# RWKV attention into soft mixture of experts, one core: r, k and v laid out in 256-byte slots, x in a rotating buffer, ku in two buffers, weight loads on another schedule

## Chip, cores, metric

One NeuronCore of a Trainium2 chip. The metric is the device time of one execution in microseconds (us); most executions of a kernel agree within a per cent or two (the kernel before took 167.73 to 170.73 us in its seven runs beside the first experiments). A run is slow when it is over 1.5% above the fastest run of the same kernel; comparisons below use fast runs. A verdict is "unclear" where the interval of the ratio leaves open whether the change is over 2%.

## The reference

Inputs are float32. For each batch b (4), head h (8) and position t (768), with 48 numbers per head:

```python
for t in range(S):
    cur = einsum('bhd,bhe->bhde', u * k[t], v[t])
    y[t] = einsum('bhd,bhde->bhe', r[t], state + cur)
    state = w * state + einsum('bhd,bhe->bhde', k[t], v[t])
x = y.transpose(0, 2, 1, 3).reshape(3072, 384)
logits = x @ phi                      # 8 experts x 4 slots = 32 columns
d = softmax over tokens; slot_input = d.T @ x
slot_out[e] = relu(slot_input[e] @ w1[e]) @ w2[e]      # 384 -> 1024 -> 384
out = softmax over slots(logits) @ slot_out
```

r, k and v are 4.7 MB each; w1 and w2 together 25 MB.

## The kernel before

Tokens go through in 24 chunks of 128 (six per batch). The program text orders each engine's work; step i does the attention of chunk i and prepares chunk i+2. The parts that matter:

```python
ld = ctx.enter_context(tc.tile_pool(name="ld", bufs=2))       # two batches in flight
def load_batch(b):
    tiles = [ld.tile([P, H, nC, D], f32, name=name, tag=name) for name, _ in srcs]
    if b > 0:                                                  # one transfer each for r, k, v
        nc.sync.dma_start(out=t[:].rearrange("p h c d -> p (h c) d"),
                          in_=src[b].rearrange("h (c p) d -> p (h c) d", p=C))
        return
    for c in range(nC): ...                                    # batch 0: one per chunk

def mults(i):
    b, c = divmod(i, nC)
    if c == 1 and 1 <= b < B - 1: load_batch(b + 1)
    nc.gpsimd.tensor_mul(rr[:, :, 0:D], r_b[:, :, c, :], W_neg[:])
    nc.gpsimd.tensor_mul(kk[:, :, 0:D], k_b[:, :, c, :], W_k3)
    ku = wk3.tile([P, H, D], f32, name="ku")                   # three buffers
    nc.gpsimd.tensor_mul(ku[:], k_b[:, :, c, :], u3)
    nc.scalar.copy(v_bf[:], v_b[:, :, c, :])                   # the cast of v

for i in range(nN + 3):
    att_a(i); mults(i + 2); trans(i + 1); att_b(i); r_copy(i + 1)   # guards cut
    xt(i - 1); disp(i - 2); att_c(i); diag(i + 1); lg(i - 1)
    ...
    for n, at in enumerate(W_AT):                              # weights, on GpSimd's queue
        if at == i: load_w(W_ORDER[n])
```

`diag` has VectorE multiply ku by r and sum it, which frees that ku buffer. `r_copy` is the last reader of a batch's r. After the steps come the experts (PE and VectorE) and the output.

The softmax here doesn't subtract the row's maximum and nothing guards it: scores larger than these inputs give would overflow.

## Time and profile before

| stage | from, us | to, us | what sets its end |
|---|---|---|---|
| batch 0, start | 0 | 24.4 | last v of batch 0 lands |
| until V1 | 24.4 | 46.8 | v of batch 1 lands |
| until V2 | 46.8 | 74.1 | v of batch 2 lands |
| until V3 | 74.1 | 106.1 | v of batch 3 lands |
| last steps | 106.1 | 135.8 | VectorE, 3.5 us per step |
| experts | 135.8 | 151.6 | PE, and the last weights |
| output | 151.6 | 168.9 | output transfers |

Measured time: 168.49 us, median of 2 runs. How to read the profile: a line of the stretch view has the stretch, its length, the busy time and instruction count of PE, its weight loads, VectorE (DVE), ScalarE (ACT) and GpSimd (POOL), then the granted PE clock, the busy share of the 16 transfer engines (over 1 where records overlap) and the GB/s written. A line of the wait view has who waited, for whom, us in total, times, and the longest. Lines of the chain are start, duration, what. SPq is SyncE issuing transfers.

### The profile page before, as it was taken

To read this page: it belongs to the slowest core of one execution; us is meant where nothing else is said; L and a number is where in the kernel's file an instruction comes from. 1 tells how busy PE (TensorE), PEld (TensorE's weight loads), DVE (VectorE), ACT (ScalarE), POOL (GpSimd) and SP (SyncE) were. 2 spreads that over 40 slices of the span, in tenths; PEclk is the share of its full clock that TensorE was granted. 3 is DMA by queue.
4 is the path that set the end of the run, shared out by engine and by line. 5 is a ranking of instruction groups with operands and counts; after the bars stand their busy time and mean duration, and the time that the engine had idled before them with its cause. 6 is when DMAs were issued, how large, how long until landed. Compare 5 with 4: busy or idle time off the path is not lost.

```text
span 168.9 us, 3607 instructions
## 1 busy us (share of the span) xinstructions
PE 86.8 (51%) x1433; PEld 65.6 (39%) x1433; DVE 93.7 (55%) x198; ACT 77.9 (46%) x163; POOL 84.2 (50%) x97
## 2 busy tenths in 40 slices
PE   0004898700037787507887810377776576844410
PEld 0003576500036665406765600265554476831000
DVE  2006889900047899607989910379999242215550
ACT  0294659200076888047777400769875400004550
POOL 2009999408912699964469794158993000000000
PEclk9999999975555799975569995589999655555555
DMA  3999999999999799999979999969999999905995
GB/s 73 200 194 193 175 207 181 197 202 222 166 165 201 157 186 196 234 206 206 215 149 189 218 216 202 200 83 140 180 146 160 204 210 204 198 15 209 353 356 201
DMA packets 48592, 32.13 MB, mean 190 GB/s; under 512 B 20160, under 2 KB 45504, under 8 KB 48576
## 3 DMA queue, kind: packets, MB, share of 16 engines
q1 hardware_dynamic: 35952, 18.88, 55.1%
q0 software_dynamic: 11520, 12.58, 46.2%
q10 hardware_dynamic: 1104, 0.44, 1.4%
q8 instruction: 11, 0.18, 0.5%
q14 instruction: 5, 0.04, 0.1%
HBM read 39.77 MB, written 4.72 MB: 263 GB/s over the span
## 4 chain that ended last, share of the span: by engine, by line
DMA 40%; SPq 24%; DVE 11%; PE 11%; ACT 5%; issue 5%; ACTq 0%; DVEq 0%
DMA v_b<-in_v_dram 32%; SPq L61 15%; SPq L66 9%; DMA out_dram<-o_s 5%; PE so_p L349 3%; PE h_p L337 3%; DMA r_b<-in_r_dram 3%; DVE at_s L210 3%; ACT t_s L196 2%; DVE o_s L381 2%; DVE sd_p L183 2%; DVE ku L179 2%; DVE dv L185 2%; ACT xt_s L257 1%; ACT r_p L173 1%
## 5 line engine op out<-in xcount | busy, mean ns | idle before, releaser
L163 POOL TENSOR_TENSOR kk<-k_b,w_rep 128x384 bf16<-128x384 f32 x24 | 24.0, 1000 | 19.2 <-PE sd_p L232 11.8
L179 DVE TENSOR_TENSOR ku<-ku,r_p 128x384 f32<-128x384 f32 x24 | 13.2, 549 | 35.4 <-ACT r_p L173 34.5
L196 ACT COPY t_s<-t_p 128x1024 bf16<-128x1024 bf16 x24 | 24.3, 1012 | 17.0 <-PE t_p L193 17.0
L210 DVE TENSOR_TENSOR at_s<-at_p,mask_ut 128x512 bf16<-128x512 f32 x48 | 30.7, 682 | 0.0
L165 POOL TENSOR_TENSOR ku<-k_b,u_rep 128x384 f32<-128x384 f32 x24 | 24.0, 1000 | 12.5 <-DVE sd_p L183 12.5
L162 POOL TENSOR_TENSOR rr<-r_b,W_neg 128x384 bf16<-128x384 f32 x24 | 24.1, 1003 | 11.6 <-ACT W_neg L100 10.5
L167 ACT CAST v_bf<-v_b 128x384 bf16<-128x384 f32 x24 | 12.1, 506 | 34.3 <-DMA v_b<-in_v_dram 34.2
L264 PE MATMUL xl_p<-phi_s,xt_s 128*128 128x32 bf16 x72 | 6.0, 186 | 39.2 <-ACT xt_s L257 39.1
L264 PEld LDWEIGHTS <-xt_s 128*128 128x128 bf16 x72 | 3.5, 101 | 41.7 <-ACT xt_s L257 41.7
L193 PE MATMUL t_p<-ident,rr 128*128 128x128 bf16 x96 | 11.6, 257 | 13.3 <-POOL rr L162 13.3
L383 ACT ACTIVATE o_s<-o_p,rsum_r 128x384 f32<-128x384 f32 x12 | 6.8, 581 | 23.5 <-PE o_p L377 17.7
L183 DVE TENSOR_REDUCE sd_p<-ku 128x8 f32<-128x384 f32 x24 | 13.5, 561 | 0.8
L185 DVE TENSOR_TENSOR dv<-v_bf,sd_p 128x384 bf16<-128x384 bf16 x24 | 13.3, 553 | 0.8
L257 ACT COPY xt_s<-xl_p 128x384 bf16<-128x384 bf16 x24 | 11.5, 481 | 4.0 <-PE xl_p L255 3.9
L193 PEld LDWEIGHTS <-rr 128*128 128x128 bf16 x96 | 6.6, 111 | 16.5 <-POOL rr L162 13.3
L244 PE MATMUL y_p<-v_bf,at_s 128*128 128x48 bf16 x192 | 12.2, 194 | 1.7 <-DVE at_s L210 1.5
L219 PE MATMUL y_p<-dv,ident 128*128 128x384 bf16 x24 | 9.7, 406 | 6.3 <-DVE dv L185 6.2
L206 PE MATMUL at_p<-t_s 64*128 64x128 bf16 x192 | 11.4, 251 | 1.2 <-ACT t_s L196 1.1
L236 DVE TENSOR_TENSOR st<-sd_p,wm 128x384 bf16<-128x384 f32 x20 | 11.0, 551 | 1.6 <-PE sd_p L232 1.5
L193 PE MATMUL t_p<-ident,kk 128*128 128x128 bf16 x96 | 11.7, 258 | 0.4 <-POOL kk L163 0.4
L246 ACT CAST x_sb<-y_p 128x384 bf16<-128x384 f32 x24 | 11.7, 486 | 0.3 <-PE y_p L244 0.3
L173 ACT COPY r_p<-r_b 128x384 f32<-128x384 f32 x24 | 11.7, 489 | 0.0
(63 smaller groups left out, 170.4 us busy)
## 6 DMA issues: line engine op xcount, KB each, us to landing
w_all<-in_moe_w_dram POOLq DMA_DIRECT2D x16, 768.0 KB, 11.2
out_dram<-o_s SPq DMA_DIRECT2D x12, 384.0 KB, 2.5
r_b<-in_r_dram SPq DMA_DIRECT2D x6, 192.0 KB, 4.9
k_b<-in_k_dram SPq DMA_DIRECT2D x6, 192.0 KB, 4.6
v_b<-in_v_dram SPq DMA_DIRECT2D x6, 192.0 KB, 4.6
w_rep<-in_w_dram ACTq DMA_DIRECT2D x1, 192.0 KB, 4.0
u_rep<-in_u_dram ACTq DMA_DIRECT2D x1, 192.0 KB, 5.7
phi_f<-in_moe_phi_dram ACTq DMA_DIRECT2D x1, 48.0 KB, 5.5
```

Source lines behind the costliest of these rows:

```text
L61: nc.sync.dma_start(out=t[:].rearrange("p h c d -> p (h c) d"), in_=src[b].rearrange("h (c p) d -> p (h c) d", p=C))
L66: nc.sync.dma_start(out=t[:, :, c, :], in_=src[b, :, c * C:(c + 1) * C, :].rearrange("h p d -> p h d"))
L162: nc.gpsimd.tensor_mul(rr[:, :, 0:D], r_b[:, :, c, :], W_neg[:])
L163: nc.gpsimd.tensor_mul(kk[:, :, 0:D], k_b[:, :, c, :], W_k3)
L165: nc.gpsimd.tensor_mul(ku[:], k_b[:, :, c, :], u3)
L173: nc.scalar.copy(r_p[:], loads[b][0][:, :, c, :])
L179: nc.vector.tensor_mul(s["ku"][:], s["ku"][:], s["r_p"][:])
L183: nc.vector.tensor_reduce(d, s["ku"][:], axis=mybir.AxisListType.X, op=ALU.add)
L185: nc.vector.tensor_mul(dv[:], s["v"][:], d[:, :, None].to_broadcast([P, H, D]))
L193: nc.tensor.transpose(t_p[:, a, q, :], s[nm][:, 2 * q:2 * q + 2, :].rearrange("p h d -> p (h d)"), ident[:])
L196: nc.scalar.copy(t_s[:], t_p[:])
L210: nc.vector.tensor_mul(at_s[:, a, :, :], at_p[a][:], mask_ut[:, None, :].to_broadcast([P, nP, P]))
```

## The change

The apparent intent: a row of 48 floats is 192 B; put each in a slot of 256 B of SBUF, the on-chip memory, so that it does not lie across a 256 B boundary. The larger load tiles need room, which comes from x (four chunks in place of 24) and from one ku buffer. The weight loads move to one per step from step 9 on.

```diff
-        tiles = [ld.tile([P, H, nC, D], f32, name=name, tag=name) for name, _ in srcs]
+        tiles = [ld.tile([P, H, nC, 64], f32, name=name, tag=name) for name, _ in srcs]
-                nc.sync.dma_start(out=t[:].rearrange("p h c d -> p (h c) d"),
+                nc.sync.dma_start(out=t[:].rearrange("p h c d -> p (h c) d")[:, :, 0:D],
-            ku = wk3.tile([P, H, D], f32, name="ku")
+            ku = wk.tile([P, H, D], f32, name="ku")          # wk has two buffers
-            nc.scalar.copy(x_sb[:, i, :], y_p[:])
+            x_t = wk4.tile([P, Dm], bf, name="x_t")          # wk4 has four
+            x_of[i] = x_t
+            nc.scalar.copy(x_t[:], y_p[:])
-        W_AT = [3, 5, 8, 10, 11, 14, 16, 17, 18, 19, 20, 21, 22, 23, 24, 24]
+        W_AT = [4, 7, 9, 10, 11, 12, 13, 14, 15, 16, 17, 18, 19, 20, 21, 22]
+    late.close()        # the load tiles' pool ends ahead of the experts
```

(Every read of r, k, v takes `0:D` of the slot; readers of `x_sb` take `x_of[i]`.)

More of the change, by code (lines that the diff above doesn't have):

```diff
@@ L50 @@
     cst = ctx.enter_context(tc.tile_pool(name="cst", bufs=1))
-    ld = ctx.enter_context(tc.tile_pool(name="ld", bufs=2))
+    late = ExitStack()
+    ld = late.enter_context(tc.tile_pool(name="ld", bufs=2))
     loads = {}
@@ L65, in load_batch @@
             for t, (_, src) in zip(tiles, srcs):
-                nc.sync.dma_start(out=t[:, :, c, :],
+                nc.sync.dma_start(out=t[:, :, c, 0:D],
                                   in_=src[b, :, c * C:(c + 1) * C, :].rearrange("h p d -> p h d"))
@@ L125 @@
     st_t = [cst.tile([P, nP, D2], bf, name=f"st{i}") for i in range(2)]
-    x_sb = cst.tile([P, nN, Dm], bf, name="x_sb")
     w1_all = cst.tile([P, E, nM, F], bf, name="w1_all")
@@ L148 @@
          tc.tile_pool(name="wk3", bufs=3) as wk3, \
+         tc.tile_pool(name="wk4", bufs=4) as wk4, \
          tc.tile_pool(name="ps", bufs=1, space=bass.MemoryType.PSUM) as ps, \
@@ L161, in mults @@
             rr, kk = rr_t[i % NB], kk_t[i % NB]
-            nc.gpsimd.tensor_mul(rr[:, :, 0:D], r_b[:, :, c, :], W_neg[:])
-            nc.gpsimd.tensor_mul(kk[:, :, 0:D], k_b[:, :, c, :], W_k3)
-            ku = wk3.tile([P, H, D], f32, name="ku")
-            nc.gpsimd.tensor_mul(ku[:], k_b[:, :, c, :], u3)
+            nc.gpsimd.tensor_mul(rr[:, :, 0:D], r_b[:, :, c, 0:D], W_neg[:])
+            nc.gpsimd.tensor_mul(kk[:, :, 0:D], k_b[:, :, c, 0:D], W_k3)
+            ku = wk.tile([P, H, D], f32, name="ku")
+            nc.gpsimd.tensor_mul(ku[:], k_b[:, :, c, 0:D], u3)
             v_bf = wk3.tile([P, H, D], bf, name="v_bf")
-            nc.scalar.copy(v_bf[:], v_b[:, :, c, :])
+            nc.scalar.copy(v_bf[:], v_b[:, :, c, 0:D])
             st8[i] = dict(rr=rr, kk=kk, ku=ku, v=v_bf)
@@ L172, in r_copy @@
             r_p = ps.tile([P, H, D], f32, name="r_p")
-            nc.scalar.copy(r_p[:], loads[b][0][:, :, c, :])
+            nc.scalar.copy(r_p[:], loads[b][0][:, :, c, 0:D])
             st8[i]["r_p"] = r_p
@@ L236, in att_b @@
                 nc.vector.tensor_mul(st_t[(i + 1) % 2][:], s_p, wm[:])
+        x_of = {}
         def att_c(i):
@@ L254, in xt @@
             for mi in range(nM):
-                nc.tensor.transpose(xl_p[:, mi * P:(mi + 1) * P], x_sb[:, i, mi * P:(mi + 1) * P], ident[:])
+                nc.tensor.transpose(xl_p[:, mi * P:(mi + 1) * P], x_of[i][:, mi * P:(mi + 1) * P], ident[:])
             xt_s = wk.tile([P, nM, P], bf, name="xt_s")
@@ L269, in disp @@
             for mi in range(nM):
-                nc.tensor.matmul(un_p[:, mi, :], x_sb[:, i, mi * P:(mi + 1) * P], Lexp[:, i, :],
+                nc.tensor.matmul(un_p[:, mi, :], x_of[i][:, mi * P:(mi + 1) * P], Lexp[:, i, :],
                                  start=(i == 0 and mi == 0), stop=False, skip_group_check=True)
```

## The prediction

A window is 256 B of SBUF starting at a multiple of 256 B; how many a row touches is counted from the addresses in the built program. That each window costs the same is the estimate from the first batch: 18.5 ns for rows with 2 windows and 13.9 for rows with 1.5 on average, 9.3 ns per window in both. The sum came to 190 us; of the 6 taken off to reach 184, 3 are for the mixed stretches and the rest for doubt. That reads may be a bound of their own is supposition, put at the 13.9 ns of the odd chunks.

> **What bounds the kernel now.** I read the page first (chain, queues), then the waits, the chain in order of time, the stretches by stage, and last the issue times of the first batch.
>
> The page says that the path runs through transfers, not through an engine: no engine is busy over 55% of the span, and the chain that ended last is DMA and its queue for 64%.
>
> ```profile
> DMA packets 48592, 32.13 MB, mean 190 GB/s; under 512 B 20160, under 2 KB 45504, under 8 KB 48576
> q1 hardware_dynamic: 35952, 18.88, 55.1%
> q0 software_dynamic: 11520, 12.58, 46.2%
> DMA 40%; SPq 24%; DVE 11%; PE 11%; ACT 5%; issue 5%; ACTq 0%; DVEq 0%
> ```
>
> q1 carries r, k, v and the output, q0 the expert weights; together they fill the 16 engines. The packet counts tell the sizes. A head's row is 192 B. Batch 0 has 3x8x768 = 18432 rows and they are nearly all of the 20160 packets under 512 B. Batches 1 to 3 have 55296 rows, yet only 25344 packets lie between 512 B and 2 KB, which is 55296/4 = 13824, plus 8192 of the second weights, 3072 output and 256 broadcast packets, exactly. So the later batches write four neighbouring rows as one 768 B packet.
>
> The wait view and the chain name the three stalls: ScalarE's cast of v for the first chunk of each batch.
>
> ```profile
> ACT v_bf L167 <- DMA v_b<-in_v_dram: 34.2, 3, 16.1
> ```
> ```profile
> 29.11 17.63 DMA v_b<-in_v_dram
> ...
> 56.97 17.08 DMA v_b<-in_v_dram
> ...
> 86.72 19.34 DMA v_b<-in_v_dram
> ...
> 142.24 1.61 issue
> ...
> 147.42 1.80 issue
> ```
>
> v lands at V1 = 46.75, V2 = 74.05, V3 = 106.06. That cast stands ahead of the copy of r of an older chunk (r_copy), which frees the buffer for the next batch; so the next r load is issued 2 us after v lands (48.76, 76.07), and batches come strictly one after the other. The two "issue" pieces are PE in the expert stage, waiting for the last weights.
>
> ```profile
> 0.00:24.40 24.40, 8.72 (x88) 6.01 (x89) 10.82 (x29) 12.28 (x22) 13.30 (x22) 1.00 1.11 172
> 24.40:46.80 22.40, 7.56 (x121) 5.83 (x119) 8.67 (x16) 5.07 (x11) 14.51 (x16) 0.76 1.09 195
> 46.80:74.10 27.30, 17.17 (x256) 13.08 (x256) 20.00 (x39) 16.60 (x36) 19.41 (x21) 0.81 1.04 191
> 74.10:106.10 32.00, 17.88 (x255) 14.18 (x255) 19.70 (x37) 16.55 (x36) 20.47 (x22) 0.71 1.11 200
> 106.10:135.80 29.70, 19.25 (x305) 14.51 (x305) 23.32 (x48) 20.67 (x46) 16.53 (x18) 0.84 1.03 159
> 135.80:151.60 15.80, 11.33 (x387) 10.89 (x388) 3.97 (x19) 0.00 (x0) 0.00 (x0) 0.50 0.96 158
> ```
>
> The reader is to see the last two columns: DMA share about 1 or above (records overlap) and about 190 GB/s in every stage up to V3. So V3 is the sum of what the engines have moved by then; after it come 29.7 us of attention bound by VectorE (a step each 3.5 us), 15.8 of experts, 17.3 of output.
>
> The first batch, one 1024-row transfer per issue of SyncE, shows what a row costs:
>
> ```profile
> 9.88 0.79 SPq L66 DMA_DIRECT2D k_b<-in_k_dram  x1
> 10.71 0.72 SPq L66 DMA_DIRECT2D v_b<-in_v_dram  x1
> 11.48 1.19 SPq L66 DMA_DIRECT2D r_b<-in_r_dram  x1
> 12.71 1.13 SPq L66 DMA_DIRECT2D k_b<-in_k_dram  x1
> 13.89 1.14 SPq L66 DMA_DIRECT2D v_b<-in_v_dram  x1
> 15.07 0.94 SPq L66 DMA_DIRECT2D r_b<-in_r_dram  x1
> 16.05 0.84 SPq L66 DMA_DIRECT2D k_b<-in_k_dram  x1
> 16.94 0.85 SPq L66 DMA_DIRECT2D v_b<-in_v_dram  x1
> ```
>
> Three fast, three slow, three fast: it goes by chunk. The landings agree: even chunks 1.18 us per transfer, odd ones 0.89, that is 18.5 and 13.9 ns per row and engine (64 rows per engine).
>
> [...] The built program puts r, k and v at addresses that leave 96 on division by 256. Even chunks then write rows at offsets 96 and 224 (both straddle: 2 windows), odd ones at 32 and 160 (1 and 2: 1.5 on average). 18.5/2 = 9.3 and 13.9/1.5 = 9.3 ns: the trace agrees with one cost per window. The later batches run at 242 packets of 768 B per us when alone, 66 ns each on 16 engines or 16.5 per row. If each row of a packet is written for itself, offsets 96, 32, 224, 160 make 7 windows, 9.4 ns each: agrees again. [...] At 66 to 68 us the trace has 151 load and 150 weight packets per us[...]; but while a first weight (2048 B packets) runs, at 36 to 39, the loads all but stop, 3 to 24 packets per us. [...] Batch 0 with 192 B packets moves 15.7 ns per row, no worse than the later batches' 16.5, so this trace shows no loss by packet size itself.
>
> **The change part by part.**
>
> 1. Slots. The intent is a row that never straddles. But 256 B slots help only if the tile starts well, and the changed program's r, k and v start at 135520, 160096, 184672 and so on: all leave 96 again. Every row then covers 96 to 288, two windows. By 9.3 ns per window, a row costs 18.6 ns everywhere. Later batches: 384 rows per engine and transfer x 18.6 = 7.14 us against 384 x 16.5 = 6.34, +0.8 x 9 transfers = +7.2 us. Batch 0: nine odd transfers x (1.18 - 0.89) = +2.6. Together +9.8 us, all in front of V3.
>
> 2. Rows per packet fall from 4 to 1 in batches 1 to 3. [...] The sum of work stays[...].
>
> 3. Weight loads by step, from 3, 5, 8, 10, 11, 14, 16, 17, 18 ... to 4, 7, 9, 10, 11, 12, ... 22. They stand in GpSimd's order behind the products of chunk step+2. Before, weights 0 to 5 and nearly all of 6 were done by V3. After, weights 4 to 8 belong to chunks 13 to 17, all of which are prepared before V3, and weight 9 follows chunk 18, whose k lands one transfer (6 to 7 us) before V3; its issue comes about 2 us after k (as at 94.58 to 96.63), so it also cuts in. A weight takes 3.7 to 3.9 us (384 packets at 103 per us, 1024 at 265). From 6.8 to 10 weights: 3.2 x 3.8 = +12 us before V3. Given back: the expert stage no longer waits, -(1.6 + 1.8) = -3.4.
>
> 4. Gap after V2. Before, weights filled the 3.7 us between v landing and first bytes of the next r. Now weight 3 goes before V2 and weight 4 is issued some 4 us after it: up to +3.5 us. Weight 0 does fill the gap after V1.
>
> 5. ku with two buffers: chunk i+2's product waits for VectorE's sum of chunk i, a step of 3.5 us before it is needed; nothing on the path. x in four buffers: overwritten by chunk i+4, last read at step i+2; no wait. Engine instructions keep shape and count (GpSimd 1.00 us, casts 0.5), as the instruction order confirms. GpSimd with a weight at each step has 3 x 0.96 + 0.95 = 3.8 us per step against 3.5 of VectorE; over the last 6 steps that is about 2 us, mostly inside its lead.
>
> Sum: 168.5 + 9.8 + 12 + 3.5 - 3.4 = 190. The mixed stretches are cheaper than added up (151/242 + 150/265 = 1.19 us of lone work per us); replayed on the kernel before, plain adding overshoots V3 by about 3 us. And weight 9 may come too late (-4)[...]. I take 184.
>
> **The rivals.**
>
> A. Rows are aligned in effect, or a slot costs one window: the write side gives 9.3 ns and the read side, at the 13.9 of the odd chunks, becomes the bound. Then 9 x 1.0 + 9 x 0.29 = -11.6 us in loads, against +12 + 3.5 - 3.4 of weights: about 169, a draw; if reads allowed 9.3 ns too, 3456 x 4.6 ns = 16 us less, about 153. For it: the intent, and a weight schedule that suits fast loads. Against it: the addresses, and the slow even chunks.
>
> B. The even-odd rhythm comes from the source address (24 KB steps per chunk). Then loads stay as they are and only the weights' order counts: 168.5 + 12 + 3.5 - 3.4 = 180.6, less the 3 for mixing, 177.
>
> C. Weights arrive early and the loads are no longer last: V3 unchanged, -3.4: 165. Against it: loads stop while weights run.
>
> **Range and chances.** Main theory 60% (176 to 194), B 20% (172 to 183), A and C 20% (153 to 172). Predicted 184 us, range 170 to 195; faster by over 2% 0.10, within 2% 0.08, slower by over 2% 0.82.
>
> **What would show it.** No 768 B load packets are left: some 41000 packets more. Load rate alone in batches 1 to 3 near 165 GB/s for step 1 (B: 186; A: over 210). The first batch loses its rhythm: all issues 1.2 us. ScalarE's wait for v grows from 34 to over 45 us, V3 goes to about 125. Ten weights land before V3 and the "issue" gaps of the expert stage are gone. I am wrong if the rows run at 14 ns or less, or if V3 stays near 106.

## The result

186.84 us (186.43 and 187.26) against 168.49: ratio 1.109, interval 1.091 to 1.127, slower. Ratios here and below are the mean time of one kernel's fast runs over that of the other's of the same rounds, so not quite the ratio of the medians quoted. The profiled run spans 184.7 us.

The page of the changed kernel: the packet counts, the queue of r, k, v and the output, and GB/s in 40 slices of 4.6 us.

```profile
GB/s 95 187 167 159 166 170 162 142 163 163 191 147 156 174 187 209 206 214 55 181 185 230 231 228 226 235 223 43 111 210 181 193 167 166 9 7 124 359 351 190
DMA packets 48593, 32.13 MB, mean 174 GB/s; under 512 B 20160, under 2 KB 45504, under 8 KB 48576
q1 hardware_dynamic: 35952, 18.88, 54.0%
```

The counts below 2 KB are those of before to the unit, and so is the queue's: loads of batches 1 to 3 still go in 768 B packets. The 55 and the 43 in the GB/s line are gaps after V2 and after V3.

The chain of the changed kernel, its three long transfers of v:

```profile
33.63 15.79 DMA v_b<-in_v_dram
...
59.23 24.36 DMA v_b<-in_v_dram
...
94.05 30.62 DMA v_b<-in_v_dram
```

Start plus duration gives V1 = 49.4, V2 = 83.6, V3 = 124.7, against 46.75, 74.05 and 106.06 (the prediction shows these lines of the kernel before). Of the 15.8 us between the two spans, 18.6 have accrued by V3, 0.6 more come in the last steps, the experts give back 3.9, and the output takes 0.5 more. The stretches, cut at those points:

```profile
0.00:27.40 27.40, 10.95 (x121) 7.89 (x121) 13.47 (x33) 14.56 (x26) 16.22 (x25) 1.00 1.12 157
27.40:49.40 22.00, 5.07 (x88) 3.77 (x86) 6.09 (x12) 3.09 (x8) 8.07 (x9) 0.69 1.04 161
49.40:83.60 34.20, 17.17 (x256) 13.08 (x256) 19.98 (x39) 16.61 (x36) 19.95 (x21) 0.75 1.08 186
83.60:124.70 41.10, 17.94 (x255) 14.21 (x255) 19.69 (x37) 16.55 (x36) 22.50 (x24) 0.67 1.08 199
124.70:155.00 30.30, 20.18 (x305) 15.33 (x305) 23.53 (x48) 20.64 (x46) 17.73 (x19) 0.78 0.99 155
155.00:166.90 11.90, 10.96 (x387) 10.73 (x388) 3.86 (x19) 0.00 (x0) 0.00 (x0) 0.50 0.16 26
```

The first two stretches are mostly loads: 157 and 161 GB/s where before had 172 and 195 (the latter with more of a weight in it), at about the same full share of the engines (1.12 and 1.04, before 1.11 and 1.09). The experts take 11.9 us at a transfer share of 0.16: the last weight lands at 158.3, and they no longer wait for one.

Loads alone, with no weight on the engines, in batch 1: first the kernel before, then the changed one.

```profile
32.00:35.00 3.00, 1.41 (x25) 1.06 (x25) 1.54 (x3) 0.00 (x0) 0.27 (x1) 1.00 1.12 187
```
```profile
37.00:43.00 6.00, 0.00 (x0) 0.00 (x0) 0.00 (x0) 0.00 (x0) 0.27 (x1) 0.50 1.11 163
```

A row's time on one engine is 192 B x 16 / rate: 16.4 ns at 187 GB/s, 18.8 at 163. The issue times of SyncE in the first batch of the changed kernel:

```profile
16.19 1.14 SPq L67 DMA_DIRECT2D r_b<-in_r_dram  x1
17.38 1.14 SPq L67 DMA_DIRECT2D k_b<-in_k_dram  x1
18.57 1.14 SPq L67 DMA_DIRECT2D v_b<-in_v_dram  x1
19.75 1.14 SPq L67 DMA_DIRECT2D r_b<-in_r_dram  x1
```

The rhythm of three fast, three slow is gone; every chunk goes at the slow pace. These are ScalarE's wait for v, summed over six waits (34.2 us before), and GpSimd's wait ahead of ku, in the changed kernel and then (ku alone) in the one before:

```profile
ACT v_bf L168 <- DMA v_b<-in_v_dram: 54.3, 6, 20.2
...
POOL ku L166 <- DVE sd_p L184: 30.6, 5, 12.0
```
```profile
POOL ku L165 <- DVE sd_p L183: 12.5, 3, 6.1
```

The second was not predicted. Its longest piece, in the order of GpSimd's work, holds back a weight (L142 issues it), which goes out only after V2:

```profile
73.79 1.00 POOL L164 TENSOR_TENSOR kk<-k_b,w_rep 128x384 bf16<-128x384 f32 x1
86.81 1.00 POOL L166 TENSOR_TENSOR ku<-k_b,u_rep 128x384 f32<-128x384 f32 x1 [12.02 <-DVE sd_p L184]
87.75 0.94 POOL L142 DMA_DIRECT2D w_all<-in_moe_w_dram  x1
```

### The profile page after: what moved, and what is told of

Its sections match the earlier page's. It is cut to its first block, busy times and chain, and to the rows that moved or that the text cites. A ratio compares the mean times of both kernels' runs of the same rounds, so it can differ in the third digit from the quotient of the medians.

```text
span 184.7 us, 3621 instructions
## 1 busy us (share of the span) xinstructions
PE 87.1 (47%) x1433; PEld 66.3 (36%) x1433; DVE 93.9 (51%) x198; ACT 78.2 (42%) x163; POOL 84.5 (46%) x97
## 2 busy tenths in 40 slices
DMA packets 48593, 32.13 MB, mean 174 GB/s; under 512 B 20160, under 2 KB 45504, under 8 KB 48576
## 4 chain that ended last, share of the span: by engine, by line
DMA 46%; SPq 23%; PE 11%; DVE 8%; ACT 6%; issue 3%; ACTq 0%; DVEq 0%
DMA v_b<-in_v_dram 38%; SPq L62 14%; SPq L67 9%; DMA out_dram<-o_s 5%; PE h_p L343 3%; PE so_p L355 3%; ACT t_s L197 3%; DMA r_b<-in_r_dram 3%; DVE at_s L211 2%; DVE o_s L387 2%; PE t_p L194 1%; DVE sd_p L184 1%; ACT xt_s L262 1%; DVE dv L186 1%; DVE ku L180 1%
## 5 line engine op out<-in xcount | busy, mean ns | idle before, releaser
L389 ACT ACTIVATE o_s<-o_p,rsum_r 128x384 f32<-128x384 f32 x12 | 6.8, 580 | 19.8 <-PE o_p L383 14.5
L194 PE MATMUL t_p<-ident,kk 128*128 128x128 bf16 x96 | 11.9, 261 | 0.4 <-POOL kk L164 0.4
L251 ACT CAST x_t<-y_p 128x384 bf16<-128x384 f32 x24 | 11.7, 486 | 0.3 <-PE y_p L247 0.3
L174 ACT COPY r_p<-r_b 128x384 f32<-128x384 f32 x24 | 11.7, 488 | 0.0
```

The lines of the kernel that those rows point to most:

```text
L194: nc.tensor.transpose(t_p[:, a, q, :], s[nm][:, 2 * q:2 * q + 2, :].rearrange("p h d -> p (h d)"), ident[:])
```

## The experiments

Theory, an estimate from the first batch of the kernel before: a row costs 9.3 ns per 256 B window it touches in SBUF, and the slots, which start at offset 96, touch two each; weights served ahead of V3 add to that. Rivals: the stride or the packets of the slots cost, not the offset; the source address makes the even-odd rhythm; the weights did it all. The first four ran on one chip, beside the kernel before (168.81 us there).

**Slots alone (a1_slots_only).** The changed kernel with the old schedule; ku still has two buffers.

```diff
-        W_AT = [4, 7, 9, 10, 11, 12, 13, 14, 15, 16, 17, 18, 19, 20, 21, 22]
+        W_AT = [3, 5, 8, 10, 11, 14, 16, 17, 18, 19, 20, 21, 22, 23, 24, 24]
```

> The slots with the old weight schedule. Window theory (each 256 B window a row touches costs 9.3 ns; all rows straddle): load packets 75 ns instead of 66, batch 0 at 1.19 us per transfer in every chunk, no rhythm; 9 x 0.85 + 9 x 0.29 = about +10 us, so 177 to 180 us. Rival (the weights did it all): 168 to 170 us, load packets at 242 per us.

Measured: 185.25 us, ratio 1.0925 (1.083 to 1.102). Loads at 213 packets per us and 1.2 us per transfer in batch 0, as expected, but some 6 us slower than expected. In the trace the transfer engines stood nearly still from 50.9 to 55.0 (share 0.02, 6 GB/s), around V1 (51.6), and the second weight was issued at 55.72 in place of 43.33. That points to ku, and led to two of the next experiments.

**Weights alone (a2_weights_only).** The kernel before with the new `W_AT`.

> The kernel before with only the new weight schedule. If the weights carry their share: V3 (landing of v of batch 3) later by two to three weights, the gaps in the expert stage gone, 174 to 178 us, loads still at 242 packets per us. If slots alone did it: 167 to 169 us.

Measured: 173.81 us, ratio 1.024 (1.016 to 1.033; slower, though unclear whether by 2%), just below the expected range; loads still at 242 packets per us. V3 is at 112.0, 6 us later; nine weights had landed by then instead of six (by bytes moved, 9.4 instead of 6.9); the experts took 10.4 us from their first to their last matmul instead of 14.2. So the schedule costs, but a third of what the prediction gave it (12 + 3.5 - 3.4). And no gap follows V2, at 73.8: with three ku buffers the weight that the changed kernel holds back is issued ahead of it, and the engines stay full from 73.8 to 78.

```profile
69.13 0.99 POOL L165 TENSOR_TENSOR ku<-k_b,u_rep 128x384 f32<-128x384 f32 x1
70.06 0.94 POOL L142 DMA_DIRECT2D w_all<-in_moe_w_dram  x1
```
```profile
73.80:78.00 4.20, 1.84 (x20) 1.49 (x21) 2.14 (x4) 3.17 (x7) 0.98 (x2) 0.50 1.17 208
```

**The changed kernel with aligned slots (a3_slots_at_0).** 160 B of padding ahead of the load tiles moves them from offset 96 to 0.

```diff
         so_r = cst.tile([P, Dm], bf, name="so_r")
+        cst.tile([P, 40], f32, name="pad")
```

> The changed kernel with 160 B of padding ahead of the load tiles, so that every slot starts at a multiple of 256 B. Window theory: one window per row to write, then reads bound at 14 ns or less per row: packets 56 ns or less (at least 285 per us), batch 0 at 0.9 us or less in every chunk; 9 x 1.8 + 18 x 0.3 = -21 us against the changed kernel, 160 to 168 us. Rival (the stride of the slots itself, or the source address, costs): no change, 185 to 188 us.

Measured: 165.34 us, ratio to before 0.968 (0.957 to 0.979); two of the four runs, the profiled one among them, slow. One unused tile takes over 20 us off the changed kernel: the straddle is the main cause, and neither the stride nor the source address.

**The kernel before with aligned rows (a4_rows_at_0).** The same padding line in the kernel before: dense rows, now at 0, 192, 128, 64.

> The kernel before with the same padding, so its dense rows lie at offsets 0, 192, 128, 64. Window theory: 1, 2, 2, 1 windows, 1.5 on average and the same in even and odd chunks: the rhythm of batch 0 goes, all at about 0.89 us, later packets 56 ns (285 per us); 9 x 0.9 + 9 x 0.29 = -10 us, 157 to 161 us. Rival (rhythm from the source address): rhythm and 168.5 us stay.

Measured: 159.53 us, ratio 0.942 (0.934 to 0.950). The rhythm of batch 0 is gone and loads run at 285 packets per us. The gain that aligned slots bring (9.1% in b2 below) is thus more than half to be had without slots. This refutes the source address, which did not move.

The next four ran together (before: 170.31 us).

**Two ku buffers alone (b1_ku2_only).** The kernel before with one line of the change.

```diff
-            ku = wk3.tile([P, H, D], f32, name="ku")
+            ku = wk.tile([P, H, D], f32, name="ku")
```

> The kernel before with ku in two buffers instead of three, nothing else. Theory 2 (two buffers of ku hold GpSimd back at each batch border, and with it the weight loads that stand behind it, so the engines' gap after V1 is no longer filled): the second weight issues after V1 instead of at 43, a gap of 3 to 4 us after V1, 171 to 175 us. Theory 1 (as in the prediction, ku is off the path): 168 to 169.5 us.

Measured: 173.26 us, ratio 1.018 (1.009 to 1.026; slower, though unclear whether by 2%). The order of GpSimd's work shows how; first this kernel, then the one before:

```profile
41.02 0.99 POOL L163 TENSOR_TENSOR kk<-k_b,w_rep 128x384 bf16<-128x384 f32 x1
49.82 1.00 POOL L165 TENSOR_TENSOR ku<-k_b,u_rep 128x384 f32<-128x384 f32 x1 [7.81 <-DVE sd_p L183]
50.76 0.80 POOL L140 DMA_DIRECT2D w_all<-in_moe_w_dram  x1
```
```profile
41.44 0.99 POOL L163 TENSOR_TENSOR kk<-k_b,w_rep 128x384 bf16<-128x384 f32 x1
42.39 0.99 POOL L165 TENSOR_TENSOR ku<-k_b,u_rep 128x384 f32<-128x384 f32 x1
43.33 0.80 POOL L140 DMA_DIRECT2D w_all<-in_moe_w_dram  x1
```

With two buffers, ku of chunk 7 waits for VectorE's sum of chunk 5, which waits for v of batch 1. The weight load behind it in program order waits as well, and the engines stand nearly still for 3.9 us around V1 (46.6):

```profile
46.10:50.00 3.90, 1.05 (x15) 0.82 (x16) 1.34 (x3) 3.17 (x7) 0.18 (x1) 0.50 0.02 6
```

V3 comes 1.2 us later than before, and the last weight, for which the experts wait, lands at 151.4 instead of 149.5.

**Slots that straddle, ku with three buffers, old schedule (b3_slots_ku3_oldw).** Room comes from one buffer less each of x and of its transpose.

```diff
-            ku = wk.tile([P, H, D], f32, name="ku")
+            ku = wk3.tile([P, H, D], f32, name="ku")
-         tc.tile_pool(name="wk4", bufs=4) as wk4, \
+         tc.tile_pool(name="wk4", bufs=3) as wk4, \
-            xt_s = wk.tile([P, nM, P], bf, name="xt_s")
+            xt_s = wk.tile([P, nM, P], bf, name="xt_s", bufs=1)
         ... and W_AT as in the kernel before
```

> Slots that straddle, old weight schedule, ku back in three buffers (room from one buffer less each of x and of its transpose, both not waited for). Theory 2: the surplus of the slots-only run goes, about +10 to +12 us of loads remain, 178 to 181 us, gap after V1 filled. Theory 1 with a larger price of the slots: stays at 184 to 186 us.

Measured: 180.91 us, ratio 1.065 (1.056 to 1.075): the slots alone, about +11 us. The gap after V1 has shrunk to 0.5 us.

**Slots at offset 64 (a5_slots_at_64).** The changed kernel with the old schedule and 224 B of padding: a row covers 64 to 256.

> Changed kernel, old weight schedule, slots at offset 64: a row ends exactly at 256. Window theory: one window, 39 ns per packet of four rows (410 per us), as at offset 0; time 150 to 160 us. Rival (it needs alignment to 256 or 128 B, or the address alone): 66 to 75 ns per packet, 175 to 185 us.

Measured: 159.01 us, ratio 0.936 (0.929 to 0.942), loads at 400 to 415 packets per us. Here a row needed no aligned start: ending at the boundary, it loads at 315 GB/s, where slots at 0 have 319 and slots at 96 have 163 (table below).

**Aligned slots, three ku buffers, old schedule (b2_slots_at_0_ku3_oldw).** The edit of b3 and the 160 B pad together.

> Slots at offset 0, old weight schedule, three buffers of ku: one window per row, and only about 7 weights before V3. V3 near 84, then 59 to 63 us: 143 to 150 us, the fastest so far. If loads were still last in every batch in spite of 39 ns per packet, 153 to 158 us.

Measured: 154.59 us, ratio 0.909 (0.901 to 0.916), correct: faster than both kernels. It misses the expected 143 to 150: V3 came at 88.7, not 84, and the experts, as before, waited for weights (1.7 and 2.4 us in the chain), whose last landed at 133.3. ScalarE's wait for v shrank from 34.2 to 18.4 us:

```profile
ACT v_bf L168 <- DMA v_b<-in_v_dram: 18.4, 2, 10.3
```

This reads as if the sum of loads and weights through to the last weight were now the bound, and not the loads up to V3; c3 and d2 below test it.

Loads alone in four kernels, one line each: dense rows at 0, slots at 64, slots at 0 with three ku buffers, and the next experiment.

```profile
25.00:26.00 1.00, 0.80 (x19) 0.59 (x16) 0.93 (x2) 1.00 (x3) 1.00 (x2) 1.00 1.10 220
```
```profile
36.50:38.00 1.50, 0.00 (x0) 0.00 (x0) 0.00 (x0) 0.00 (x0) 0.00 (x0) 0.50 1.08 315
```
```profile
37.00:39.00 2.00, 0.00 (x0) 0.00 (x0) 0.00 (x0) 0.00 (x0) 1.98 (x3) 0.50 1.10 319
```
```profile
37.00:40.00 3.00, 0.00 (x0) 0.00 (x0) 0.00 (x0) 0.00 (x0) 2.74 (x4) 0.50 1.28 262
```

| rows in SBUF | windows per row | GB/s | ns per row and engine | ns per window |
|---|---|---|---|---|
| slots at 96 (changed) | 2 | 163 | 18.8 | 9.4 |
| dense at 96 (before) | 1.75 | 187 | 16.4 | 9.4 |
| dense at 0 | 1.5 | 220 | 14.0 | 9.3 |
| slots at 64 | 1 | 315 | 9.8 | 9.8 |
| slots at 0 | 1 | 319 | 9.6 | 9.6 |

One cost per window, 9.3 to 9.8 ns, fits all five. Windows of 128 B do not fit: dense rows at 0 would then cost the same as slots at 0 (two windows for every row in both), and they took 14.0 ns against 9.6.

Batch 0 is not in the table, and does not follow it. From v of one chunk to v three chunks on, nine transfers, SyncE took 0.89 us per transfer with slots at 0 (issues at 10.17 and 18.16) and 0.92 with dense rows at 0 (9.94 and 18.19): about 14 ns per row with 1 window and with 1.5. Something other than the windows sets this pace; what, no run shows.

**Source rows 256 B apart (c1_source_256).** b2 with a wrong result: the source address steps 64 floats per partition, so that source rows don't straddle either.

```diff
-                                  in_=src[b].rearrange("h (c p) d -> p (h c) d", p=C))
+                                  in_=bass.AP(tensor=src.tensor, offset=src.offset + b * H * S * D,
+                                              ap=[[64, P], [5696, nC * H], [1, D]]))
         ... and batch 0 likewise
```

> Slots at offset 0, three ku buffers, old weights, and a wrong result on purpose: rows are read from source addresses 256 B apart instead of 192 B, so each source row lies in one window too. If only the window on the write side counts: still about 400 to 415 packets per us, 39 ns, and about 154 us. If the straddling source rows (1.5 windows on average) held part of the 39 ns: over 430 packets per us.

Measured: 157.45 us (ratio 0.935, 0.927 to 0.942, beside another set of runs of the kernel before), loads at 262 GB/s where b2 has 319: slower than b2, not equal and not faster. The packets changed, which neither expectation had:

```profile
DMA packets 90064, 32.13 MB, mean 209 GB/s; under 512 B 75456, under 2 KB 86976, under 8 KB 90048
```

75456 - 20160 = 55296: each row of batches 1 to 3 now is a packet of 192 B. So the 768 B packets of the other kernels go by the source, where rows of neighbouring tokens lie side by side, and neighbouring tokens go to neighbouring partitions; the layout in SBUF did not change the count (20160 packets under 512 B with dense rows, with slots at 96 and with slots at 0). A single-row packet costs 11.7 ns where a row of a joint packet costs 9.6. Whether a straddling source row costs anything stays open, because the edit changed both. Why batch 0 goes in 192 B packets, although its source rows lie side by side too, is open as well.

**One weight earlier (c3_one_weight_earlier, d1_slots_at_0_again, d2_one_earlier_again).** c3 is b2 with `W_AT = [3, 5, 6, 8, 10, 11, 14, 16, 17, 18, 19, 20, 21, 22, 23, 23]`; then b2 (d1) and c3 (d2) again side by side.

> Slots at offset 0, three ku buffers, old weight schedule with one weight more issued at step 6, where the engines have some 4 us of idle time between 42 and 57 us, and the two last ones at step 23. If the end is set by the sum of the engines' work: last weight lands 2 to 4 us earlier, 151 to 153 us. If the earlier weight only delays v of batch 2: 154 to 158 us.

Measured: 151.04, 151.29, 154.07 and 162.77 us, the latter two slow; ratio of the fast ones to before 0.895, unclear.

> The same kernel as the aligned one with three ku buffers and the old schedule, again, beside the next on the same chip: 153 to 156 us.

Measured: 155.65 us, ratio 0.920 (0.915 to 0.925).

> The same kernel with one weight at step 6, whose profile fell in the slow state the first time. If the idle time of the engines was worth a weight: 1.5 to 3 us faster than its neighbour, last weight landing 2 to 4 us earlier. If the first difference was chance: within 1 us.

Measured: 154.86 us median; the six runs are 150.43 and five from 153.36 to 155.17, which count as slow because of the one at 150.43. The earlier weight is not shown to help. The profiles do show the last weight landing at 132.4 us instead of 136.2, as expected; the times point the same way, but fast against fast rests on one run.

## Why the prediction was right

Time (184 against 186.84) and direction held, and so did the main mechanism, slots that straddle. Of the other four steps two were wrong, one was over-priced, and one came true for another reason. By its steps:

1. **Slots.** Held. Predicted +9.8 us from 18.6 ns per row; measured 18.8 ns and, alone, +11.0 (6.5% of 170). The load rate it named, near 165 GB/s, is 163; V3, named at about 125, is 124.7. Rival A needed aligned addresses; given those by padding, the rows of batches 1 to 3 took 9.6 ns, the lower of its two cases, and not the 13.9 of the other. Rival B fell with the padded kernel before.
2. **Rows per packet fall from 4 to 1.** Wrong. The counts stayed, and some 41000 further packets never came. That four rows go in one packet follows the source (c1); what a packet costs follows the offsets of its rows in SBUF, 163 to 319 GB/s with the same packets. The 7 windows for four rows fit the table, at 9.4 ns each. The trace of the kernel before has 151 load and 150 weight packets per us with 768 B weight packets, 3 to 24 load packets with 2048 B ones, and no run shows why.
3. **Weights.** Right in kind, too large in size: +12 and -3.4, so +8.6, against +4.1 measured alone (2.4% of 169). The count was nearly right: by bytes, 9.8 weights had moved by V3 in the changed kernel and 9.4 in the weights-only run, against 6.9. The price was not: there, 2.5 weights of 3.8 us moved V3 by 6.0 us. Stretches in which loads and weights run together, allowed 3 us in the sum, may be the rest; it was not taken apart. The return in the experts, -3.4 predicted, is -3.9 in the stretches.
4. **Gap after V2.** It came, 2.4 us without a packet (84.6 to 87.0), but not from the schedule. The weight that could have filled it stood behind a ku that waited 12.0 us for one of its two buffers. From the kk before it, an estimate without that wait is issue at about 75.7, 8 us ahead of V2; in the weights-only run, same schedule with three buffers, it went ahead of V2 and there was no gap. So this gap belongs to step 5, and that 3.5 us was near is luck. No run has the whole change with three ku buffers; this is read from the two traces.
5. **ku off the path.** Wrong. The step looked at who needs ku, and not at what stands behind it in GpSimd's order: a weight load. Alone it costs +3.0 us (1.8% of 170), with its gap at V1; in the changed kernel another weight is under way there, and the gap lies after V2. C, that weights come early and loads are not last, is refuted by the weights-only run.

Two of its readings of batch 0 were also less than they seemed. The odd chunks' 13.9 ns, divided by 1.5 windows, gave the same 9.3 ns as the even ones; but rows of one window were no faster there (see below the table), so that agreement proves little. And its own 18.5 and 13.9 ns average to 16.2 per row, not 15.7; that packet size costs nothing is not borne out by 11.7 against 9.6 ns in c1.

The sum came out near in part by luck: weights 4.5 us too high, slots 1 too low, a gap of 3.5 put down to the schedule where ku alone costs 3.0, and 6 taken off for mixing and doubt. Measured parts multiply to 1.065 x 1.018 x 1.024 = 1.110, against 1.109 for the whole change; since the gap of ku lies elsewhere in the whole, the match is closer than the parts warrant.

## What to carry to other kernels

Here padding an inner dimension to 256 B helped only where the tile's base lay well (9.6 and 9.8 ns per row at offsets 0 and 64, 18.8 at 96): read the base address out of the built program, and check whether rows cross a multiple of 256. One unused 160 B tile was worth 5.8% in the kernel before, and with slots and three ku buffers 14.5% (180.91 to 154.59 us); the aligned slots came out 9.1% and, run again, 8.0% below the kernel before, while slots on the wrong base cost 6.5%. When a buffer count is cut to make room, look at everything behind the new wait in that engine's order, transfers above all.
